# The second product by seven multiplications from block 42 instead of 50, its weight sums made in place and for four experts sooner

## The chip, the cores and the metric

The kernel runs on one core of a Trainium2 chip. The metric is the device time of one execution in microseconds (us); of several runs the median is given. The core has a matrix engine (TensorE, PE in the profile; its weight loads are listed apart as PEld), a vector engine (VectorE, DVE), an activation engine (ScalarE, ACT), a general engine (GpSimd, POOL) and a queue processor (SyncE, SP). SP and ACT issue most transfers, POOL the scatters by index.

## The reference

Two stages follow each other. The first is a mixing over the sequence by Fourier transform; the second sends each token to one of eight experts by a hash of its number.

```python
batch, seq, dim = (8, 2496, 256)
X = np.fft.rfft(x, axis=1)
y = np.fft.irfft(X * (filt_r + 1j * filt_i)[None], n=seq, axis=1)     # 8 x 2496 x 256, fp32
x = y.reshape(19968, 256)
expert = token_ids * 2654435761 % 8
for e in range(8):                                                   # w1: 256 x 1024, w2: 1024 x 256
    out[expert == e] = np.maximum(x[expert == e] @ w1[e], 0) @ w2[e]
```

All is fp32.

## The kernel before

**Tiles of tokens.** Tokens are sorted by expert while they are produced: the Fourier part scatters each row of its result to a place in a DRAM buffer `xs`, and every 256 places there (one tile, one expert) make one *block* of the second part. There are 85 tiles; 80 are always used (`NSURE`), 5 more only if the counts need them. The order of the tiles is fixed in five stages, since a tile can only be read when the batches are done from which its tokens come: blocks 0 to 9 need the first two batches, 10 to 19 three, 20 to 29 four, 30 to 49 six, 50 to 79 all eight. Within a stage even blocks go through one half of the experts and odd blocks through the other, so that an expert's weights, kept in one of two sets, mostly serve several blocks of the same parity; they are loaded again only where the expert changes (a condition on the transfer).

**A block** (`step`) computes a hidden tile of 1024 x 256 and an output tile of 256 x 256. The first product, `up` (line 881), is made by seven multiplications of half-size pieces instead of eight. For this POOL makes four differences of weight pieces for the block after (`weight_sums`, line 872, four subtractions), DVE makes four differences of token pieces (`token_sums`). The second product, `down` (line 918), is an ordinary product of 16 matmul calls of 256 columns. From block `WS` = 50 on, `late_step` (line 1047) takes the place of this with `both` (line 930): seven multiplications for the second product too, each of four matmul calls of 128 columns. Two names stand for the PE work of the two ways: rows `dps` at line 923 are `down`, rows `dne`, `dna`, `dnb`, `dnc` at line 950 are the seven. A matmul call of fp32 shows as two instructions.

**Sums of the second weights.** The seven multiplications need four 128 x 512 pieces per expert made from `w2`. `prepare(e, part)` (line 203) makes them once for each expert, on POOL, long before: part 0 loads `w2[e]` (1 MB) on SP into a buffer `raw` of the pool `xp`, which has two buffers and also serves the x tiles; parts 1 to 4 are four subtractions on POOL (row `mid<-raw`, line 199), from `raw` into a part of the tile `mid`; part 5 writes the result (1 MB) on SP to the DRAM buffer `t2s`. Blocks from `WS` on load them back with their weights (line 469), into the tiles `d_t` and `e_t`, the tables of the Fourier part, which are free once its last middle stage is over; `both` also keeps its token pieces and its sums `s` in the tile of the filter.

**The Fourier part** goes on beside the blocks. A batch has three parts, cut into pieces: `stage1` (loads x, first transform), `forward` and `back` (middle, with the filter), `stage3` (last transform, whose rows POOL scatters to `xs`, four scatters a piece). Their loads are `load1`, `load2`, `load4` on SP, their writes to DRAM are issued by ACT. A list `todo` gives each piece a due time in blocks; `run_until(t)` issues what is due, at five points of a block: after `up`, at three points inside `down`, and at the end. In a block from 50 on it is not called, since nothing is left by then. A stage 3 piece is eight matmuls of 256 columns, two ACT copies and four scatters on POOL.

**Order and waits.** Each engine and each queue runs its instructions in the order in which they stand. POOL's order in a block is: the weight differences for the block after, the two scatters of the block before (`store`, line 1012), then what `run_until` brings. SP's order has the loads of w1 (line 464) and w2 (line 467) two blocks ahead, and between them the loads of the pieces. Token tiles (`load`, line 836: four transfers `xg`, one `no`) are issued by ACT. In the built program SP's and ACT's transfers take eight semaphores in turn, and the issue of a transfer waits until the previous one with its semaphore has landed, whichever queue issued that.

```python
for e in range(E):
    t = 34.3 + 1.5 * e
    todo += within([(t + d, lambda e=e, k=k: prepare(e, k)) for k, d in enumerate((0, 1.1, 1.4, 1.7, 2, 2.3))])
```

`within` moves the due time into the second half of its block.

Of the kernel before, what the change touches and what calls it, by code (L numbers as in the profile page):

```python
# [11 lines left out]
F32 = mybir.dt.float32  # L12
# [7 lines left out]
P = 128  # L20
B, S, C = 8, 2496, 256
# [26 lines left out]
FP = F // P  # L48
# [2 lines left out]
NPAD = NT * TB - N  # L51
NQP = NPAD // P
NSURE = NT - 5
WS = 50

# [68 lines left out]
def kernel(  # L126
# [10 lines left out]
    nc = tc.nc  # L137
# [9 lines left out]
    t2_dram = nc.dram_tensor("t2s", (E, P, FP * C), F32)  # L147

    def pool(stack, name, bufs, space=None):
        kw = {} if space is None else {"space": space}  # L150
        return stack.enter_context(tc.tile_pool(name=name, bufs=bufs, **kw))
# [5 lines left out]
    xpool = pool(ctx, "xp", 2)  # L157
    ppool = pool(ctx, "pp", 3)
    t4pool = pool(ctx, "t4", 2)
# [16 lines left out]
    mid = cpool.tile([P, 10, SG * C], F32)  # L176
# [21 lines left out]
    def minus(eng, out_, a, b, op=OP.subtract):  # L198
        eng.tensor_tensor(out_, a, b, op=op)

    raw = {}

    def prepare(e, part):

        to = mid[:, 5 + 2 * (e % 2):7 + 2 * (e % 2), :].rearrange("p a b -> p (a b)")
        if part == 0:
            raw[e] = xpool.tile([P, FP, C], F32, name=f"raw_{e}", tag="x")
            nc.sync.dma_start(out=raw[e][:], in_=moe_w2[e].rearrange("(fp p) c -> p fp c", p=P))
        elif part < 5:
            b11, b12, b21, b22 = [raw[e][:, 4 * f:4 * f + 4, P * c:P * c + P] for f in range(2) for c in range(2)]  # L210
            t = [to.rearrange("p (k f c) -> p k f c", k=4, c=P)[:, k] for k in range(4)]
            k = part - 1
            minus(nc.gpsimd, t[k], (b12, b22, b22, b21)[k], (b11, t[0], b12, t[1])[k])
        else:
            nc.sync.dma_start(out=t2_dram[e], in_=to)

    put_off = {2: [], 3: []}

# [227 lines left out]
    def weights(i, which):  # L446

        if i >= NT:
            return
        if i >= 2 and which == 0:  # L450
            ws[i] = ws[i - 2][0:2]
        eng, kw = nc.sync, {}
        if which == 0:
            ws[i].append(eng.value_load(chunk_i[0:1, 0, i:i + 1], min_val=0, max_val=E - 1))
            if i >= 2:
                ws[i].append(eng.value_load(chunk_i[0:1, 1, i:i + 1], min_val=0, max_val=1))
        e = ws[i][2]
        if i >= 2:
            kw = {"cond": ws[i][3]}
        if which == 0:  # L460


            for f in (slice(0, F // 2), slice(F // 2, F)) if i < 2 else (slice(0, F),):
                eng.dma_start(out=ws[i][0][:, :, f],
                              in_=moe_w1[bass.ds(e, 1)].rearrange("one (p dp) f -> p (one dp) f", p=P)[:, :, f], **kw)
        else:
            eng.dma_start(out=ws[i][1], in_=moe_w2[bass.ds(e, 1)].rearrange("one (fp p) d -> p (one fp) d", p=P), **kw)
            if WS <= i < NSURE:
                eng.dma_start(out=late["t2"][i % 2].rearrange("p k f c -> p (k f c)"),
                              in_=t2_dram[bass.ds(e, 1)].rearrange("one p k -> p (one k)"), **(kw if i >= WS + 2 else {}))  # L470

# [254 lines left out]
    def within(todo, share=.5):  # L726

        return [(t // 1 + .5 + t % 1 * share, piece) for t, piece in todo if t is not None]
# [69 lines left out]
    todo = [(t - 200, piece) for t, piece in head]  # L798
    todo += [(t, lambda k=k: pads(k)) for k, t in enumerate((10.9, 11.6, 11.9, 16.9, 17.6, 17.95, 22.9))]

    def batch(b, t1, t2, t3):

        a1, a2, a3 = spaced(*t1, NU), spaced(*t2, N_2), spaced(*t3, NU)
        x0, d0, e0 = t1[0] - 2.5, t2[0] - 1.2, t3[0] - 1.2
        out = part2(b, a2, [max(d0, a2[2 * g] - 2.2) for g in range(NS // SG)], .6)
        out += part3(b, a3, [max(e0, a3[2 * v] - 2.2) for v in range(NV)])
        if b > 2:
            out += part1(b, a1, [max(x0, a1[2 * v] - 2.5) for v in range(NV)])
        return out
# [3 lines left out]
    todo += part2(3, spaced(6.4, 10, N_2), [5.2, 5.4, 5.6, 6.5, 7.5], .6)  # L813
    todo += part3(3, spaced(12, 16, NU), [11.2, 11.4, 12.5])
    todo += batch(4, (7.5, 11), (12.4, 16.4), (18.3, 22.3)) + batch(5, (13, 17), (18.4, 21.6), (23.2, 26.8))
    todo += batch(6, (20, 24), (26, 32), (34, 40)) + batch(7, (29, 34), (35.5, 40), (41.6, 47))
    for e in range(E):
        t = 34.3 + 1.5 * e
        todo += within([(t + d, lambda e=e, k=k: prepare(e, k)) for k, d in enumerate((0, 1.1, 1.4, 1.7, 2, 2.3))])
    todo.sort(key=lambda t: t[0])  # L820
    pre = [t for t in todo if t[0] < 0]
    main = [t for t in todo if t[0] >= 0]
# [107 lines left out]
    def both(i, ht):  # L930

        w1, w2 = ws[i][0:2]
        x, st, t = parts[i], parts[i]["sums"], sums[i]
        t2, s, one = late["t2"][i % 2], late["sums"], late["one"]
        h11, h12, h21, h22 = [ht[:, h, 4 * f:4 * f + 4, :] for h in range(2) for f in range(2)]
        b11, b12, b21, b22 = [w2[:, 4 * f:4 * f + 4, P * c:P * c + P] for f in range(2) for c in range(2)]
        half = F // 2

        def bank(k, name):
            p, tag = (banks[k], k) if k in banks else (fps, "f")  # L940
            return p.tile([P, 4, P], F32, name=f"{name}_{i}", tag=tag)

        def product(ps, w, xx, first):
            for f in range(4):
                nc.tensor.matmul(out=ps[:, f, :], lhsT=w[:, f * P:(f + 1) * P], rhs=xx,  # L945
                                 start=first and f == 0, stop=True, skip_group_check=True)

        def second(ps, a, b, first):
            for f in range(4):
                nc.tensor.matmul(out=ps[:, 0, :], lhsT=a[:, f, :], rhs=b[:, f, :],  # L950
                                 start=first and f == 0, stop=True, skip_group_check=True)

        def relu(out, in_):
            nc.scalar.activation(out=out, in_=in_, func=AF.Relu)  # L954

        def plus(out, ps, other):
            nc.vector.tensor_tensor(out, ps, other, op=OP.add)  # L957

        a, b, c = [bank(k, "up" + k) for k in "abc"]
        g, e = bank("f", "upg"), bank("f", "upe")  # L960
        if i + 1 < NSURE:
            token_parts(i + 1, late["xt"][i % 2])
        product(a, w1[:, 0, 0:half], x[0, 0], True)
        nc.scalar.copy(out=h21, in_=a[:])
        ask(i)
        product(b, t[1], st[:, 1, :], True)
        plus(h12, b[:], h21)
        product(g, t[2], st[:, 2, :], True)
        plus(h21, g[:], h12)
        product(c, t[0], st[:, 0, :], True)  # L970
        plus(h22, c[:], h21)
        relu(h22, h22)
        product(e, t[3], x[1, 1], True)
        plus(h21, e[:], h21)
        relu(h21, h21)
        product(a, w1[:, 1, 0:half], x[0, 1], False)
        relu(h11, a[:])
        minus(nc.vector, s[:, 0], h21, h22, OP.add)
        product(c, w1[:, 1, half:], st[:, 3, :], False)
        plus(h12, c[:], h12)  # L980
        relu(h12, h12)
        weights(i + 2, 0)

        e, a = bank("b", "dne"), bank("d", "dna")
        b, c = bank("f", "dnb"), bank("f", "dnc")
        rows[i] = outs.tile([P, 2, C], F32, name=f"osb_{i}", tag="osb") if i + 1 < NSURE else late["last"]
        o11, o12, o21, o22 = [rows[i][:, h, P * k:P * k + P] for h in range(2) for k in range(2)]
        second(e, h22, t2[:, 3], True)
        second(c, s[:, 0], t2[:, 0], True)
        second(a, h11, b11, True)  # L990
        nc.scalar.copy(out=one, in_=a[:, 0, :])
        minus(nc.vector, s[:, 1], s[:, 0], h11)
        minus(nc.vector, s[:, 2], h11, h21)
        minus(nc.vector, s[:, 3], h12, s[:, 1])
        second(b, s[:, 1], t2[:, 1], True)
        if i + 1 < NSURE:
            token_sums(i + 1, late["st"][i % 2], range(2))
        plus(o22, c[:, 0, :], one)
        plus(o21, e[:, 0, :], one)
        plus(o12, b[:, 0, :], one)  # L1000
        second(a, h12, b21, False)
        nc.scalar.copy(out=o11, in_=a[:, 0, :])
        if i + 1 < NSURE:
            token_sums(i + 1, None, range(2, 4))
        second(b, s[:, 2], t2[:, 2], False)
        plus(o22, b[:, 0, :], o22)
        plus(o21, b[:, 0, :], o21)
        second(c, s[:, 3], b22, False)
        plus(o12, c[:, 0, :], o12)
        weights(i + 2, 1)  # L1010
# [32 lines left out]
    def run_until(t):  # L1043
        while main and main[0][0] < t:
            main.pop(0)[1]()
# [9 lines left out]
    def step(i):  # L1055
        if i >= WS:
            late_step(i)
# [74 lines left out]
```

## Time and profile before

| | us |
|---|---|
| median of 3 runs (1415.62 to 1419.44) | 1417.82 |
| the profiled execution, its own time | 1415.08 |
| span of the profiled execution, first to last instruction | 1413.3 |
| start of block 0 (ACT copies its first product) | 140.2 |
| start of block 26, 42, 50 | 646.2, 916.4, 1029.8 |
| a block of the first kind with nothing of the Fourier part in it (47, 48, 49) | 13.16 |
| a block of the second kind (51 and later) | 12.51 |

The beginning of a block is read at one instruction, ACT's copy of the first product (line 899, or 964 in a block of the second kind), so the time from one to the next is one block. The engines are busy for these shares of the span: PE 97%, PEld 90%, DVE 63%, POOL 59%, ACT 29%. Sections of the page that follow name, for each group of instructions, its line, engine and operand tiles, its count, its total and mean duration, and what ended the idle time before it. A view by stretches gives the busy times of all engines between two moments, with the share of time in which the 16 DMA engines moved data.

### The profile page before, as it was taken

The numbers are of one execution on the slowest core, as the hardware profiler recorded it, in microseconds if no ns is written. First come the engines' busy times: TensorE is split into PE (matmuls) and PEld (weight loads), VectorE is DVE, ScalarE is ACT, GpSimd is POOL, SyncE is SP. The second block draws the span as 40 slices with busy tenths as digits, with TensorE's granted clock in tenths as the row PEclk, the third lists the DMA queues.
The fourth block names the chain that finished last, engine by engine and source line by source line (L and its number), as shares of the span: only waits on it lengthen the run. The fifth ranks groups of instructions, "written<-read, shape, count | busy, mean of one in ns | idle before, by whom it ended". The sixth has DMA issues, their size and how long they took to land.

```text
span 1413.3 us, 26363 instructions
## 1 busy us (share of the span) xinstructions
PE 1369.3 (97%) x9426; PEld 1271.4 (90%) x9426; DVE 891.9 (63%) x1636; ACT 416.0 (29%) x760; POOL 828.0 (59%) x736
## 2 busy tenths in 40 slices
PE   8999899999999999999999999999999999999997
PEld 7777888988888988899999899999999999999997
DVE  7773584575556576445765477657666777676775
ACT  4554122223232223232222222222222222222222
POOL 6267243743665565587533687798855556655563
PEclk9999999999999999999999999999999999999999
DMA  8677854867887698888755775887732525161621
GB/s 227 208 239 224 246 177 121 284 198 242 252 266 228 188 308 271 250 282 260 228 164 141 222 252 181 238 240 239 257 119 74 184 75 192 42 223 40 215 46 35
DMA packets 244505, 278.33 MB, mean 197 GB/s; under 512 B 125171, under 2 KB 213670, under 8 KB 234948
## 3 DMA queue, kind: packets, MB, share of 16 engines
q1 hardware_dynamic: 95149, 179.33, 40.2%
q10 hardware_dynamic: 129303, 52.69, 15.4%
q0 software_dynamic: 19920, 44.59, 9.0%
q8 instruction: 77, 1.26, 0.4%
q14 instruction: 56, 0.46, 0.1%
HBM read 293.65 MB, written 86.15 MB: 269 GB/s over the span
## 4 chain that ended last, share of the span: by engine, by line
PE 82%; DMA 8%; DVE 4%; issue 2%; ACT 1%; POOL 1%; ACTq 1%; SPq 0%; POOLq 0%; DVEq 0%
PE dps L923 20%; PE up_b L888 8%; PE up_a L888 5%; PE up_c L888 5%; PE pd L267 4%; PE dnc L950 4%; PE dnb L950 4%; PE dna L950 4%; PE upc L945 4%; PE upa L945 4%; PE pb L312 4%; PE pa L267 3%; PE pc L335 3%; PE upe L945 2%; PE upb L945 2%
## 5 line engine op out<-in xcount | busy, mean ns | idle before, releaser
L923 PE MATMUL dps<-wts,ht 128*128 128x256 f32 x1600 | 367.0, 380 | 1.5 <-ACT ht L892 1.5
L923 PEld LDWEIGHTS dps<-wts,ht 128*128 128x128 f32 x1600 | 302.0, 190 | 44.8 <-ACT ht L892 2.7
L1015 POOL DMA_INDIRECT out_dram<-osb,no x158 | 165.2, 1045 | 221.5 <-DVE osb L957 142.7
L433 POOL DMA_INDIRECT xs<-o,sidx x176 | 176.3, 1002 | 163.6 <-ACT o L269 68.4
L878 POOL TENSOR_TENSOR tw<-wts 128x512 f32<-128x512 f32 x158 | 204.1, 1292 | 111.3 <-DMA wts<-in_moe_w_dram 87.1
L878 POOL TENSOR_TENSOR tw<-wts,tw 128x512 f32<-128x512 f32 x158 | 205.8, 1303 | 6.2
L895 DVE TENSOR_TENSOR ht<-up_b,ht 128x512 f32<-128x512 f32 x150 | 103.6, 691 | 116.9 <-PE up_b L888 91.8
L892 ACT ACTIVATE ht<-ht 128x512 f32<-128x512 f32 x150 | 94.3, 630 | 185.2 <-DVE ht L895 165.3
L322 DVE TENSOR_TENSOR z<-pb,filt 64x512 f32<-64x512 f32 x160 | 110.2, 689 | 26.9 <-PE pc L335 24.9
L928 DVE COPY osb<-dps 128x512 f32<-128x512 f32 x50 | 34.5, 691 | 145.5 <-PE dps L923 145.2
L888 PE MATMUL up_a<-xt,wts 128*128 128x128 f32 x800 | 114.8, 276 | 7.3 <-ACT ht L899 4.0
L888 PEld LDWEIGHTS up_a<-xt,wts 128*128 128x128 f32 x800 | 105.2, 192 | 11.0 <-ACT ht L899 4.9
L888 PE MATMUL up_b<-st,tw 128*128 128x128 f32 x800 | 107.7, 278 | 3.8 <-DVE ht L895 2.5
L888 PEld LDWEIGHTS up_b<-st,tw 128*128 128x128 f32 x800 | 98.1, 193 | 6.3 <-issue 5.7
L895 DVE TENSOR_TENSOR ht<-up_c,ht 128x512 f32<-128x512 f32 x100 | 69.0, 690 | 37.5 <-PE up_c L888 32.9
L954 ACT ACTIVATE ht<-ht 128x512 f32<-128x512 f32 x90 | 56.5, 630 | 120.6 <-DVE ht L957 75.1
L338 ACT COPY mid<-pc 128x512 f32<-128x512 f32 x60 | 35.0, 583 | 155.0 <-PE pc L335 97.0
L267 PE MATMUL pd<-t,wi_t 120*117 120x256 f32 x320 | 75.9, 379 | 3.3 <-DMA t<-d 3.3
L318 DVE TENSOR_TENSOR y<-pb,filt 128x512 f32<-128x512 f32 x80 | 55.1, 689 | 34.1 <-PE pb L312 31.8
L323 DVE TENSOR_TENSOR y<-y,z 128x512 f32<-128x512 f32 x80 | 73.6, 920 | 2.7
L312 PE MATMUL pb<-mid,d_t 128*128 128x256 f32 x280 | 72.9, 383 | 1.5 <-DVE z L322 1.5
L269 ACT COPY o<-pd 117x512 f32<-117x512 f32 x80 | 44.9, 584 | 99.3 <-PE pd L267 48.7
(210 smaller groups left out, 2426.2 us busy)
## 6 DMA issues: line engine op xcount, KB each, us to landing
wts<-in_moe_w_dram SPq DMA_DIRECT2D x162, 1024.0 KB
xg<-xs ACTq DMA_DIRECT2D x321, 64.0 KB
mid<-d SPq DMA_DIRECT2D x70, 256.0 KB
d<-mid ACTq DMA_DIRECT2D x60, 256.0 KB
d_t<-t2s SPq DMA_DIRECT2D x15, 1024.0 KB
e_t<-t2s SPq DMA_DIRECT2D x15, 1024.0 KB
x<-in_x_dram SPq DMA_DIRECT2D x39, 312.0 KB
t<-d SPq DMA_DIRECT2D x12, 960.0 KB
```

Source lines behind the costliest of these rows:

```text
L267: nc.tensor.matmul(out=ps[0:cols * H, k, :], lhsT=w[:], rhs=src[:, 2 * i + k, :], start=True, stop=True)
L312: nc.tensor.matmul(out=ps[:, i, :], lhsT=d_t[:, s, :], rhs=rhs, start=True, stop=True)
L322: nc.vector.tensor_tensor(out=z[b], in0=ps[a], in1=f_t[1][64 * hi:64 * hi + 64, s1:s1 + 2, :], op=OP.mult)
L433: st = nc.gpsimd.indirect_dma_start(out=xs[:], out_offset=bass.IndirectOffsetOnAxis(ap=index, axis=0), in_=rows, in_offset=None, bounds_ch ...
L878: eng.tensor_tensor(t[k][:], p, q, op=OP.subtract)
L888: nc.tensor.matmul(out=ps[bank][:, f, :], lhsT=w[:, f * P:(f + 1) * P], rhs=xx, start=first and f == 0, stop=True, skip_group_check=True)
L892: nc.scalar.activation(out=out, in_=in_, func=AF.Relu)
L895: nc.vector.tensor_tensor(out, ps[bank][:], other, op=OP.add)
L923: nc.tensor.matmul(out=ps[:, h, :], lhsT=ht[:, h, fp, :], rhs=w2[:, fp, :], start=(fp == 0), stop=(fp == FP - 1))
L945: nc.tensor.matmul(out=ps[:, f, :], lhsT=w[:, f * P:(f + 1) * P], rhs=xx, start=first and f == 0, stop=True, skip_group_check=True)
L950: nc.tensor.matmul(out=ps[:, 0, :], lhsT=a[:, f, :], rhs=b[:, f, :], start=first and f == 0, stop=True, skip_group_check=True)
L1015: st = nc.gpsimd.indirect_dma_start(out=out[:], out_offset=bass.IndirectOffsetOnAxis(ap=to_rows[i][:, h:h + 1], axis=0), in_=o[:, h, :], i ...
```

## The change

- `WS` goes from 50 to 42: blocks 42 to 49 become blocks of the second kind.
- `prepare` works in place. The four quarters of `w2[e]` are loaded into one buffer by four transfers of 256 KB instead of one of 1 MB, the four subtractions overwrite the buffer, and the result is written from it. Nothing goes through `mid`.
- For experts 0 to 3 the buffer comes from the pool `t4` (two buffers, used for stage 3), and they are due from 26.4 on, 1.2 blocks apart; experts 4 to 7 use `xp` and are due from 33.4 on, 1.3 blocks apart. Before, all eight were due from 34.3 on, 1.5 apart.
- Batch 6's middle is due at 25.5 to 31.5 (before 26 to 32), its stage 3 at 33.6 to 39.6 (34 to 40); batch 7's stage 1 at 28.5 to 33 (29 to 34), its middle at 34 to 38.8 (35.5 to 40), its stage 3 at 40.6 to 46.6 (41.6 to 47).
- `both` calls `run_until(i + 1)` between its first and its second product, so that the stage 3 pieces due in blocks 42 to 45 run there.

```diff
-WS = 50
+WS = 42
@@ def prepare(e, part):
-        to = mid[:, 5 + 2 * (e % 2):7 + 2 * (e % 2), :].rearrange("p a b -> p (a b)")
         if part == 0:
-            raw[e] = xpool.tile([P, FP, C], F32, name=f"raw_{e}", tag="x")
-            nc.sync.dma_start(out=raw[e][:], in_=moe_w2[e].rearrange("(fp p) c -> p fp c", p=P))
+            p = t4pool if e < 4 else xpool
+            raw[e] = p.tile([P, FP, C], F32, name=f"raw_{e}", tag="t4" if e < 4 else "x")
+            w = raw[e][:].rearrange("p k c -> p (k c)").rearrange("p (k f c) -> p k f c", k=4, c=P)
+            src = moe_w2[e].rearrange("(fp p) c -> p fp c", p=P)
+            for k, (f, c) in enumerate(((0, 0), (1, 1), (0, 1), (1, 0))):
+                nc.sync.dma_start(out=w[:, k], in_=src[:, 4 * f:4 * f + 4, P * c:P * c + P])
         elif part < 5:
-            b11, b12, b21, b22 = [raw[e][:, 4 * f:4 * f + 4, P * c:P * c + P] for f in range(2) for c in range(2)]
-            t = [to.rearrange("p (k f c) -> p k f c", k=4, c=P)[:, k] for k in range(4)]
-            k = part - 1
-            minus(nc.gpsimd, t[k], (b12, b22, b22, b21)[k], (b11, t[0], b12, t[1])[k])
+            w = raw[e][:].rearrange("p k c -> p (k c)").rearrange("p (k f c) -> p k f c", k=4, c=P)
+            to, p, q = ((0, 2, 0), (2, 1, 2), (1, 1, 0), (3, 3, 1))[part - 1]
+            minus(nc.gpsimd, w[:, to], w[:, p], w[:, q])
         else:
-            nc.sync.dma_start(out=t2_dram[e], in_=to)
+            w = raw[e][:].rearrange("p k c -> p (k c)").rearrange("p (k n) -> p k n", k=4)
+            nc.sync.dma_start(out=t2_dram[e].rearrange("p (k n) -> p k n", k=4), in_=w)
...
-    todo += batch(6, (20, 24), (26, 32), (34, 40)) + batch(7, (29, 34), (35.5, 40), (41.6, 47))
+    todo += batch(6, (20, 24), (25.5, 31.5), (33.6, 39.6)) + batch(7, (28.5, 33), (34, 38.8), (40.6, 46.6))
     for e in range(E):
-        t = 34.3 + 1.5 * e
-        todo += within([(t + d, lambda e=e, k=k: prepare(e, k)) for k, d in enumerate((0, 1.1, 1.4, 1.7, 2, 2.3))])
+        t = 26.4 + 1.2 * e if e < 4 else 33.4 + 1.3 * (e - 4)
+        todo += within([(t + d, lambda e=e, k=k: prepare(e, k)) for k, d in enumerate((0, 1.1, 1.3, 1.5, 1.7, 1.9))])
@@ def both(i, ht):
         weights(i + 2, 0)
+        run_until(i + 1)
```

## The prediction, made before the changed kernel was run

> **What bounds the kernel now.** I read four views in this order: the page's shares and its chain that ended last, the stretches block by block, the chain inside single blocks, and the timeline where a block is longer than its matmuls.
>
> ```profile
> PE 1369.3 (97%) x9426; PEld 1271.4 (90%) x9426; DVE 891.9 (63%) x1636; ACT 416.0 (29%) x760; POOL 828.0 (59%) x736
> ...
> PE 82%; DMA 8%; DVE 4%; issue 2%; ACT 1%; POOL 1%; ACTq 1%; SPq 0%; POOLq 0%; DVEq 0%
> ```
>
> PE is at 97%, its weight loads at 90%, and 82% of the chain is PE. Most of the 8% of DMA lies before block 0 (140 us). Inside the blocks the kernel is a queue of matmuls, so a change pays by the matmul time it removes and by the waits of PE it removes or makes. The stretches below are blocks 27, 28, 29, 33, 43, 49, 50 and 51.
>
> ```profile
> 663.16:679.71 16.55, 16.55 (x106) 15.31 (x105) 11.89 (x19) 4.13 (x7) 10.88 (x10) 1.00 0.67 224
> 679.71:694.60 14.89, 14.89 (x98) 13.86 (x97) 9.15 (x15) 3.55 (x6) 6.80 (x6) 1.00 0.89 267
> 694.60:714.77 20.17, 20.17 (x123) 18.40 (x122) 13.76 (x19) 6.47 (x11) 8.60 (x9) 1.00 0.49 149
> ...
> 765.76:782.53 16.77, 16.10 (x108) 14.34 (x106) 5.75 (x11) 3.48 (x8) 7.90 (x7) 1.00 0.78 227
> ...
> 931.31:946.20 14.89, 14.89 (x99) 13.77 (x98) 7.86 (x12) 4.04 (x7) 13.23 (x13) 1.00 1.00 278
> 1016.64:1029.80 13.16, 13.16 (x91) 12.33 (x90) 6.01 (x12) 2.96 (x5) 4.53 (x5) 1.00 0.81 280
> 1029.80:1043.08 13.28, 12.72 (x114) 12.53 (x113) 10.16 (x21) 3.50 (x7) 8.28 (x8) 1.00 0.52 179
> 1043.08:1055.59 12.51, 12.51 (x114) 12.51 (x113) 8.56 (x21) 3.50 (x8) 7.32 (x7) 1.00 0.18 42
> ```
>
> After the length come the busy times of PE, PEld, DVE, ACT and POOL, then clock, DMA share and GB/s. A block of the first kind with nothing beside it is 13.16, of the second kind 12.51, both without a gap on PE. Block 43 holds one stage 3 piece more: 14.89 - 13.16 = 1.73 for 8 matmuls, 0.216 each, though DMA is at 1.00. With that price I can tell how much of blocks 26 to 41 is waiting: 916.42 - 646.22 = 270.2 long, 16 x 13.16 = 210.6 for the blocks, 260 Fourier matmuls x 0.216 = 56.2, so 3.4 remain. Of these, 2.7 lie in block 33 (16.77 against 13.16 + 4 x 0.216). Blocks 42 to 49 have 0.3, block 50 has 0.77 (13.28 against 12.51).
>
> ```profile
> 774.92 7.62 DMA xg<-xs
> 782.53 0.59 ACT ht L899
> ...
> 1007.86 0.89 PE up_b L888 x8
> 1008.75 6.91 PE dps L923 x32
> 1015.66 0.89 PE up_a L888 x8
> ```
>
> The lower lines give the removed work: `down` is 6.91, one product of 8 instructions is 0.89. The upper ones are block 33: ACT made its copy at 782.53, after an `xg` transfer. In the order of instructions with their waits, what stood ahead of that copy is the issue of `no` for tile 36, and it waits for a semaphore that SP's load of w1 for block 35 holds (1 MB, issued 770.32). ACT issued `no` at 782.10, and PE stood meanwhile. I call this a **hold**: a transfer of ACT queued behind a large one of SP. Its price here is 2.7.
>
> ```profile
> 1034.66 1.27 POOL L878 TENSOR_TENSOR tw<-wts,tw 128x512 f32<-128x512 f32 x1
> 1034.71 1.76 DVE L199 TENSOR_TENSOR filt<-ht 128x512 f32<-128x512 f32 x1 [0.70 <-ACT ht L954]
> ...
> 1036.52 0.97 PEld L950 LDWEIGHTS dnc<-d_t,filt 128*128 128x128 f32 x8 [0.75 <-DVE filt L199]
> ```
>
> Block 50's 0.77: the first sum of `both` took 1.76 on DVE, beside a subtraction on POOL, where the same row's median is 0.69, and `dnc` waited for it.
>
> **What the Trainium skill says.** "Perfetto Trace Analysis", Identifying the Most-Contended Engine: judge TensorE by weight loads, not matmul occupancy. The trace agrees: PEld goes from 12.33 of 13.16 to 12.51 of 12.51, and the block shrinks although PE reads full in both. "SBUF — State Buffer", Who interferes with whom: a DVE instruction with two SBUF inputs contends with a GpSimd instruction that reads SBUF, and one blocks. The 1.76 against 0.69 fits. "DMA: Bandwidth & Descriptors", Issuing engines are not separate DMA queues: all queues run on the same 16 engines. Block 33 shows ACT's issue waiting on SP's load, though by a semaphore of this program.
>
> **The change, part by part.**
>
> *Blocks 42 to 49.* Each loses 6.91 and gains seven times 0.89 = 6.24; the measured blocks give 13.16 - 12.51 = 0.65. Eight blocks: **-5.2**, all of it on the path, since PE has no gap in either kind. Their DVE rises from 6.01 to about 9 of 12.51: hidden.
>
> *Stage 3 pieces inside `both`.* Same 1.73 of PE, now between the products. ACT's two copies (0.585 each) come in 3.5 of 12.5 busy. POOL then has 4 x 1.29 differences, 2 stores and 4 scatters at 1.30 (their spacing in the timeline): 13.0 in a block of 12.51 + 1.73 = 14.24. It fits by 1.2, and its differences serve the next block, so lateness of some us is free. `run_until` also issues the last t4 load (block 42) on SP ahead of w2 for block 44, which has a block and a half: 0.
>
> *Start of the second kind.* The 0.77 leaves block 50. In block 42 the same sum has the 1.73 of the stage 3 piece ahead of `dne`, more than the 1.07 it was late. It can come back at block 46, the first without a piece. Half of it counted: **-0.4**.
>
> *In-place sums.* 32 subtractions before and after; the row `mid<-raw` has 1.26 to 1.61 each. Contiguous operands may gain nothing or up to 0.3 each; POOL in blocks 26 to 33 had 6 to 14 busy of 15 to 20. Taken as 0, at worst covered by that idle time. SP issues 24 transfers more at 0.41: 9.8 over 13 blocks, against waits of hundreds of us on SP: 0 by itself. The bytes are the same, the rows half as long. Price of one expert: load and store are 2.1 MB; queue 1 moved 179.33 MB in 40.2% of 1413.3, 316 GB/s, so 6.6 of all 16 engines; if the load went only as fast as queue 10 with its small packets (52.69 MB in 15.4%, 242 GB/s), 7.7. I take 6.6.
>
> *Experts 0 to 3 sooner.* 26.6 of DMA goes into blocks 27 to 31, 86.9 us with a mean share of 0.63: 0.63 + 0.31 = 0.94. Block 43 ran free at 1.00, so a full DMA alone doesn't stop PE; late transfers would. What waits there: SP stands before each store until POOL's last subtraction (before: 47.3 us in 6 waits, up to 16.9), with weights two blocks ahead and loads of batches 6 and 7 behind it; the buffers of experts 2 and 3 also wait for the stores of 0 and 1. These loads have about a block of slack. Every transfer issue from here on gets another of the eight semaphores: the hold in block 33 is probably gone (its `no` no longer stands behind a w1 load), others can arise, with ACT's `xg` and batch writes now behind quarters of `raw`. From below nothing, from above the rivals. I take -2.7 at one half, **-1.3**, and **+0.7** for a fuller DMA.
>
> *Second weight sums loaded sooner.* Experts change at blocks 44, 46, 47, 48, 50 and 51 (from the tokens); with the first two, 8 loads in place of 2: 6.3 MB, 20 of DMA in blocks 40 to 49. But some 3.6 experts' preparation leaves these blocks, 24. Nothing.
>
> *Earlier due times of batches 6 and 7.* Matmuls only change their block: 0. The shortest distance is batch 7's `load2` right behind its last stage 1 piece (blocks 32.9 and 32.6): SP stands there some us until the write has landed (estimated from the scatters of `o`, which land 2.9 to 5.0 after their issue), the first use is over a block later.
>
> Sum: -5.2 - 0.4 - 1.3 + 0.7 = **-6.2**. The profiled execution would take 1415.08 - 6.2 = 1408.9. It lies 2.7 below the median of the runs, so from the median: 1417.82 - 6.2 = **1411.6**. What a measurement of this kernel can tell from no change is about 0.3%, 4.25 us.
>
> **Rivals.**
>
> *DMA too full in blocks 27 and 28.* 0.67 + 0.31 and 0.89 + 0.31: the second goes over by 0.2 x 14.9 = 3.0, and one hold more comes with it (2.7, against the sum's 1.3 + 0.7 - 2.7). For it: blocks 22 and 23 at 0.93 and 0.97 lost 0.4. Against it: block 29 has room (0.49), and block 43. Gain about 6.2 - 3.0 - 1 = 2: 1415.8, no change that can be told.
>
> *The port between POOL and DVE.* If POOL stays late after the scatters, its differences meet DVE's sums in blocks 46 to 49 too: 4 x 0.77 = 3.1 lost, gain 3.1, 1414.7. Against it: 1.2 of room in each of blocks 43 to 45.
>
> *Holds at the preparations; slower.* The place is ACT's queue in blocks 28 to 40: its `xg`, `d1` and `d2` transfers are behind `raw` quarters and stores that wait for POOL. If half of the eight experts make one hold as in block 33, 4 x 2.7 = 10.8 stands against 6.2: 1422.4. It decides from three holds (8.1) on. Against it: before, eight preparations in blocks 34 to 47, with SP waits of up to 16.9, cost under 1.5 in all, since an `xg` is issued a half to a whole block after the load that it waits for.
>
> **How the numbers follow.** Forecast 0.72, DMA 0.17, port 0.05, slower 0.06. If every wait from 26 to 50 goes, 5.2 + 0.77 + 3.4 + 0.3 = 9.7: 1408.1, the low end. The first two rivals end at 1415.8; with one us for their rough prices the high end is 1417. Faster 0.72, within 0.22, slower 0.06.
>
> **What would show it.** Right: blocks 46 to 49 at 12.51, 43 and 44 at 14.24, block 42 without 0.77, row `dps` x1344 in place of x1600, `dnc` of 42 to 45 not waiting. Wrong in its main term: blocks 43 to 49 longer than this, with PE idle before `dnc` or `dnb`. The rivals: idle of PE in blocks 27 to 40 with ACT released by `xg`, or DMA at 1.0 over several blocks; `filt` sums of 1.7 in blocks 46 to 49.

## The result, and the profile after

| | before, us | after, us |
|---|---|---|
| median of 20 runs each, taken together | 1417.96 | 1414.01 |
| lowest to highest | 1412.63 to 1425.16 | 1407.74 to 1418.50 |
| span of the profiled execution | 1413.3 | 1411.7 |
| start of block 26, 42, 50 | 646.22, 916.42, 1029.80 | 647.30, 921.23, 1027.59 |

The ratio of the times is 0.9972, with a 95% interval of 0.996 to 0.9984: some 4 us faster, where 6.2 were forecast. Two later sets ran the changed kernel again and gave 0.9956 (0.9943 to 0.9969) and 0.9982 (0.997 to 0.9995). The forecast of 1411.6 is 2.4 us low; the measured time lies inside the range.

From the page of the changed kernel, the shares, the chain that ended last, and the row of the ordinary second product:

```profile
PE 1367.1 (97%) x9618; PEld 1273.8 (90%) x9618; DVE 907.8 (64%) x1708; ACT 419.4 (30%) x776; POOL 831.4 (59%) x736
...
PE 79%; DMA 10%; DVE 6%; issue 3%; POOL 1%; ACT 1%; ACTq 0%; SPq 0%; POOLq 0%; DVEq 0%
...
L926 PE MATMUL dps<-wts,ht 128*128 128x256 f32 x1344 | 312.2, 381 | 3.0 <-ACT ht L895 3.0
```

Row `dps` has x1344, as the change says: eight blocks fewer with 32 instructions each. PE still has 97%. What is new is DVE's share of the chain, 6% where it was 4%: in some place matmuls now wait for DVE.

The stretches show where. They are blocks 27, 28, 29, 33, 35, 36, 43, 49, 50 and 51 of the changed kernel; the columns are those explained in the prediction.

```profile
665.04:682.52 17.48, 17.48 (x114) 16.25 (x113) 13.93 (x19) 4.13 (x7) 14.16 (x12) 1.00 0.88 293
682.52:699.53 17.01, 16.33 (x99) 14.69 (x99) 9.84 (x15) 4.49 (x8) 7.95 (x7) 1.00 0.89 285
699.53:717.82 18.29, 18.29 (x114) 16.80 (x113) 13.25 (x19) 5.20 (x9) 13.89 (x12) 1.00 0.98 296
768.00:782.95 14.95, 14.95 (x99) 13.85 (x98) 5.84 (x12) 4.04 (x8) 4.85 (x5) 1.00 0.67 190
801.29:820.61 19.32, 18.52 (x114) 16.69 (x113) 16.46 (x20) 5.19 (x10) 13.87 (x12) 1.00 0.59 181
820.61:840.12 19.51, 18.57 (x114) 16.74 (x113) 16.93 (x21) 5.00 (x9) 16.51 (x14) 1.00 0.87 255
935.41:949.65 14.24, 14.24 (x122) 13.97 (x121) 9.84 (x22) 4.46 (x10) 12.16 (x12) 1.00 0.73 223
1015.09:1027.59 12.50, 12.50 (x114) 12.50 (x113) 8.19 (x20) 3.49 (x7) 7.26 (x6) 1.00 0.90 295
1027.59:1040.66 13.07, 12.78 (x114) 12.59 (x114) 9.79 (x21) 3.50 (x8) 7.27 (x7) 1.00 0.63 202
1040.66:1053.16 12.50, 12.50 (x114) 12.50 (x113) 8.79 (x21) 3.49 (x7) 7.29 (x7) 1.00 0.19 44
```

Block 43 has 14.24 and block 49 has 12.50, both without a gap on PE: this is the intended gain, in full. In blocks 35 and 36 PE stands for 0.8 and 0.9 us, while DVE is busy for 16.46 and 16.93. A block with the same matmuls in the kernel before, block 36 there, has 18.29 with DVE busy for 12.72:

```profile
813.58:831.87 18.29, 18.29 (x114) 16.77 (x113) 12.72 (x19) 5.10 (x10) 15.60 (x14) 1.00 0.75 249
```

DVE has hardly more work, 20 and 21 instructions in these two stretches against 19. Single instructions of it take longer.

The timeline of the changed kernel inside block 36 (start, duration, engine, line, operation; in brackets the idle time before it and what ended that) shows which ones:

```profile
821.00 1.02 POOL L436 DMA_INDIRECT xs<-o,sidx  x1 [4.41 <-issue]
...
824.92 0.99 POOL L436 DMA_INDIRECT xs<-o,sidx  x1 [0.30 <-issue]
...
825.92 1.31 POOL L199 TENSOR_TENSOR raw<-raw 128x512 f32<-128x512 f32 x1
...
827.16 1.29 POOL L881 TENSOR_TENSOR tw<-wts 128x512 f32<-128x512 f32 x1
...
827.31 1.30 DVE L872 TENSOR_TENSOR st<-xt 128x128 f32<-128x128 f32 x1
...
828.53 1.27 POOL L881 TENSOR_TENSOR tw<-wts,tw 128x512 f32<-128x512 f32 x1
828.64 1.30 DVE L872 TENSOR_TENSOR st<-st,xt 128x128 f32<-128x128 f32 x1
...
829.76 1.31 POOL L881 TENSOR_TENSOR tw<-wts 128x512 f32<-128x512 f32 x1
829.87 1.35 DVE L872 TENSOR_TENSOR st<-xt 128x128 f32<-128x128 f32 x1
...
831.03 1.31 POOL L881 TENSOR_TENSOR tw<-wts,tw 128x512 f32<-128x512 f32 x1
831.14 1.36 DVE L872 TENSOR_TENSOR st<-xt,st 128x128 f32<-128x128 f32 x1
...
832.42 0.68 DVE L321 TENSOR_TENSOR y<-pb,filt 128x512 f32<-128x512 f32 x1
833.11 1.39 DVE L325 TENSOR_TENSOR z<-pb,filt 64x512 f32<-64x512 f32 x2
...
834.65 1.09 PE L270 MATMUL pd<-t,wi_t 120*117 120x256 f32 x4 [0.94 <-DVE z L325]
```

Read it from above. The block began at 820.61, and POOL begins it with the four scatters of the stage 3 piece of block 35 (the first and the last are shown). So its weight differences `tw` start at 827.16, and there they meet DVE's four token sums `st`. Each `st` begins just after a `tw` and ends about 0.15 after it: 1.30 to 1.36 instead of the 0.29 that it has alone. The four take some 4 us more. Behind them on DVE stand `y` and `z`, the filter steps of a `forward` piece, which read a PSUM buffer that PE wants for `pd`; PE stands 0.94. (ACT too stands in this block, 8.22 before a copy at 836.01, behind `xg`. But it stands 7.88 in the same place, at 838.52, in block 36 of the kernel without these waits that is shown below.)

How far all blocks 26 to 41 are affected follows from the prediction's own sum: after, they take 921.23 - 647.30 = 273.9; less 16 x 13.16 and 264 Fourier matmuls x 0.216 there remain **6.3 us of waiting, where before had 3.4**. (Before there were 260. Eight came from blocks 42 to 49, and four left for block 25.)

### The profile page after: what moved, and what is told of

Same layout as the page of the kernel before. It is cut to its first block, busy times and chain, and to the rows that moved or that the text cites. A ratio compares the mean times of both kernels' runs of the same rounds, so it can differ in the third digit from the quotient of the medians.

```text
span 1411.7 us, 26945 instructions
## 1 busy us (share of the span) xinstructions
PE 1367.1 (97%) x9618; PEld 1273.8 (90%) x9618; DVE 907.8 (64%) x1708; ACT 419.4 (30%) x776; POOL 831.4 (59%) x736
## 3 DMA queue, kind: packets, MB, share of 16 engines
q8 instruction: 79, 1.29, 0.4%
## 4 chain that ended last, share of the span: by engine, by line
PE 79%; DMA 10%; DVE 6%; issue 3%; POOL 1%; ACT 1%; ACTq 0%; SPq 0%; POOLq 0%; DVEq 0%
PE dps L926 16%; PE up_b L891 6%; PE dnc L953 5%; PE dna L953 5%; PE dnb L953 5%; PE upa L948 5%; PE upc L948 4%; PE up_a L891 4%; PE pd L270 4%; PE up_c L891 4%; PE pb L315 3%; PE pa L270 3%; PE pc L338 3%; PE upe L948 2%; PE upb L948 2%
## 5 line engine op out<-in xcount | busy, mean ns | idle before, releaser
L926 PE MATMUL dps<-wts,ht 128*128 128x256 f32 x1344 | 312.2, 381 | 3.0 <-ACT ht L895 3.0
L926 PEld LDWEIGHTS dps<-wts,ht 128*128 128x128 f32 x1344 | 255.0, 191 | 40.5 <-ACT ht L895 3.6
L898 DVE TENSOR_TENSOR ht<-up_b,ht 128x512 f32<-128x512 f32 x126 | 87.1, 692 | 98.6 <-PE up_b L891 75.5
L891 PE MATMUL up_a<-xt,wts 128*128 128x128 f32 x672 | 97.3, 278 | 5.5 <-DVE xt L859 3.6
L891 PEld LDWEIGHTS up_a<-xt,wts 128*128 128x128 f32 x672 | 89.1, 193 | 8.4 <-issue 3.8
L891 PE MATMUL up_b<-st,tw 128*128 128x128 f32 x672 | 90.3, 278 | 3.7 <-DVE ht L898 2.7
L891 PEld LDWEIGHTS up_b<-st,tw 128*128 128x128 f32 x672 | 82.4, 193 | 5.8 <-issue 5.6
L953 PE MATMUL dna<-wts,ht 128*128 128x128 f32 x608 | 80.4, 275 | 0.0
L948 PE MATMUL upa<-filt,wts 128*128 128x128 f32 x592 | 78.2, 275 | 0.0
L199 DVE TENSOR_TENSOR filt<-ht 128x512 f32<-128x512 f32 x76 | 57.4, 756 | 26.4 <-ACT ht L957 26.4
```

The source lines that it names most:

```text
L891: nc.tensor.matmul(out=ps[bank][:, f, :], lhsT=w[:, f * P:(f + 1) * P], rhs=xx, start=first and f == 0, stop=True, skip_group_check=True)
L898: nc.vector.tensor_tensor(out, ps[bank][:], other, op=OP.add)
L926: nc.tensor.matmul(out=ps[:, h, :], lhsT=ht[:, h, fp, :], rhs=w2[:, fp, :], start=(fp == 0), stop=(fp == FP - 1))
```

## The experiments

The theory: the new due time of batch 6's stage 3, 33.6, puts every piece at .80 of its block, where 34 put it at .50, right behind `up`: the first is due at 33.80 instead of 34.50. The four scatters then run over the end of the block, POOL's differences start late, meet `st`, and PE waits. The rivals: the seven products from block 42 on cause it, POOL simply has too much work beside, or the in-place preparation costs it.

The first four kernels ran in a set in which the kernel before took 1457.97 (median of 43) and its first part alone is some 15 us longer; only ratios and blocks of that set are compared with each other.

### Batch 6's stage 3 back behind `up`

```diff
-... batch(6, (20, 24), (25.5, 31.5), (33.6, 39.6)) ...
+... batch(6, (20, 24), (25.5, 31.5), (34, 40)) ...
```

> The changed kernel with batch 6's stage 3 due at 34 to 40 as before, so that its pieces fall at .50 of a block (right behind the first product) and not at .80. Theory (phase): in the changed kernel the four scatters of a piece issued at .80 run over the block's end, POOL's weight differences start some 5 us late and meet DVE's token sums (row st, 1.2 to 1.35 us each in blocks 34 to 38 against 0.29 before); z and y come late and PE waits about 1 us in each of blocks 35 to 38. Then here st is back at 0.29 between 785 and 880 us, blocks 35 to 38 lose less than 1 us together instead of 4.3, and the time is 0.994 to 0.996 of before, against 0.9972 of the changed kernel. Rival (POOL has too much to do): the four subtractions for an expert every 1.3 blocks in place of 1.5 overfill POOL, whatever the phase: st stays above 1 us and blocks 35 to 38 lose 3 us or more. Rival (DMA): the waits come from a fuller DMA and stay as they are.

Measured: 1448.08, ratio to before 0.9941 (0.9917 to 0.9965). Blocks 35, 36, 37 and 38 take 18.28, 18.34, 20.08 and 17.85. Over blocks 33 to 41 it takes 150.46; the kernel of the next experiment, with the same pieces there and the late due time, takes 153.51. The `st` of blocks 34 to 38 (count: shortest, median and longest in ns), first one of three rows of this kernel, whose other two have medians of 292 and 283:

```profile
L872 DVE TENSOR_TENSOR st<-xt x10: 282/288/357, 820.9 to 895.9; 128x128 f32<-128x128 f32 x10
```

then the changed kernel, in its own set:

```profile
L872 DVE TENSOR_TENSOR st<-xt x10: 283/1216/1356, 789.6 to 868.0; 128x128 f32<-128x128 f32 x10
L872 DVE TENSOR_TENSOR st<-st,xt x5: 293/1241/1314, 790.0 to 866.8; 128x128 f32<-128x128 f32 x5
L872 DVE TENSOR_TENSOR st<-xt,st x5: 284/1354/1357, 790.4 to 869.3; 128x128 f32<-128x128 f32 x5
```

With only these due times undone, no `st` of this window is slow and the blocks are short. The theory held. All of POOL's work is still in this kernel, so its amount alone does not make the waits.

### The ordinary second product up to block 49

```diff
-WS = 42
+WS = 50
```

(an edit of the changed kernel)

> The changed kernel with WS back at 50: sums in place and sooner, due times of batches 6 and 7 as changed, but blocks 42 to 49 of the first kind. Theory: the eight blocks are worth 8 x 0.65 = 5.2 us and the rest of the change costs 1 to 2 us (hold in block 33 gone, -2.7; 4.3 in blocks 35 to 38, 0.9 each in 27 and 40), so this kernel is 1 us slower than before: ratio 0.9995 to 1.002. If instead the blocks brought less than their matmuls say, it stands at the changed kernel's 0.997 to 0.9985; if the earlier schedule is harmless, at 0.998 to 0.9995.

Measured: 1453.45, 0.9984 (0.9964 to 1.0004). The number missed: I had 0.9995 to 1.002, and 0.9984 lies where I had put a harmless schedule. The interval reaches into all the ranges named, so the number decides nothing. The blocks gave the answer that was asked for: blocks 46 to 49 have 13.16 again, while blocks 35 and 36 keep their 19.55 and 19.49, and `st<-xt` has a median of 1169 ns. So the new waits are not from the seven products, but from the earlier schedule.

### No subtractions for experts 4 to 7

```diff
         elif part < 5:
+            if e >= 4:
+                return
```

> The changed kernel without the four subtractions for experts 4 to 7 (their sums are left out; loads and stores stay). Phase theory: the scatters still run over the block's end and POOL's differences still begin about 4 us into the block, so part of the meeting with st stays: st medians 0.6 to 1.3 us between 785 and 880, blocks 35 to 38 lose 1.5 to 3.5 us. Rival (too much work on POOL): st is back at 0.29 and blocks 35 to 38 lose under 1 us. In both, the store of expert 7's sums no longer waits for POOL, so the wait of PE in block 40 for the stage 3 load behind it on SP (0.9) goes.

Measured, one run: 1448.66. The wait of block 40 is gone (14.89, as expected). Blocks 35 to 38, however, have 19.54, 20.25, 20.78 and 17.30, and blocks 33 to 41 take 154.49: no better than with all subtractions. So less work on POOL does not give the time back. But my theory's number was exceeded too, and its trace is not the same picture: here most `st` escape, as the rival had it,

```profile
L874 DVE TENSOR_TENSOR st<-xt x10: 277/292/1352, 820.7 to 899.7; 128x128 f32<-128x128 f32 x10
```

and the chain runs over ACT, whose copies stand behind transfers:

```profile
860.09 8.28 DMA d<-mid
...
871.25 1.08 ACT o L274 x2
872.33 0.50 ACT ht L904
...
872.87 0.71 PE up_a L893 x4
```

With the late pieces, taking away one wait let another one stand in its place. That the late phase costs is common to all kernels that have it. That it costs by `st` is what the traces of most of them show, not of this one, and no run separates `st` from everything else that the phase moves.

### Both stage 3 behind `up`

The first experiment, and batch 7 in the same manner:

```diff
-    ... (33.6, 39.6)) + batch(7, (28.5, 33), (34, 38.8), (40.6, 46.6))
+    ... (34, 40)) + batch(7, (28.5, 33), (34, 38.8), (41, 47))
```

> The changed kernel with batch 6's stage 3 due at 34 to 40 and batch 7's at 41 to 47, so that every stage 3 piece falls at .50. Theory (phase): as with batch 6's alone, blocks 34 to 40 lose under 1 us in place of about 5, st between blocks 34 and 39 is at 0.29; besides, the load for batch 7's first stage 3 piece is issued 0.2 block later and used 0.7 block later, so the 0.9 that PE waited for it in block 40 goes. Together 3.5 to 5 us faster than the changed kernel: 0.993 to 0.9955 of before, and 0.996 to 0.998 of the changed kernel beside it. If the phase only moved the waits elsewhere, it is within 1 us of the changed kernel.

> The kernel with both stages 3 at .50 a second time, beside the changed kernel, because the two medians of the last set (1412.02 of 7 runs, 1411.99 of 22) did not show the 3.2 us by which its trace is shorter from block 25 to 52. Phase theory: blocks 25 to 52 again 3 us shorter than in the changed kernel, 0.992 to 0.996 of before, 0.997 to 0.999 of the changed kernel. Rival (the blocks' gain is given back elsewhere): the trace shows the 3 us lost again before block 25 or after block 52, and the medians are equal within 1 us.

Measured twice: 0.995 (0.9929 to 0.9971; median 1412.02 against 1417.15) and 0.9944 (0.9927 to 0.9962; 1411.37 against 1419.08). The timeline of block 36, which begins here at 822.09, is the counterpart of the one shown above:

```profile
819.77 1.27 POOL L881 TENSOR_TENSOR tw<-wts 128x512 f32<-128x512 f32 x1
...
823.92 1.26 POOL L881 TENSOR_TENSOR tw<-wts,tw 128x512 f32<-128x512 f32 x1
...
828.80 0.32 DVE L872 TENSOR_TENSOR st<-xt 128x128 f32<-128x128 f32 x1
829.15 0.29 DVE L872 TENSOR_TENSOR st<-st,xt 128x128 f32<-128x128 f32 x1
...
830.77 1.01 POOL L436 DMA_INDIRECT xs<-o,sidx  x1 [1.82 <-ACT mid L341]
...
834.69 0.99 POOL L436 DMA_INDIRECT xs<-o,sidx  x1 [0.30 <-issue]
```

The differences end at 825.2, before `st` starts; the scatters come after it and end at 835.7, inside the block. The chain of the first of the two executions through blocks 35 to 38 is all but wholly PE (issue 0.3%). The waiting in blocks 26 to 41, by the same sum as above, is 2.6 and 3.3.

### The changed kernel again, for the comparison within one set

> The changed kernel once more, beside the others on the same chip: 0.996 to 0.9985 of before, with blocks 35 to 38 again some 4 us over their matmuls and st above 1 us there, if these waits belong to the kernel's order and not to one execution.

> The changed kernel beside it, a third time: 0.995 to 0.9985 of before, and 3 us longer from block 25 to 52 than the kernel with both stages 3 at .50.

Measured: the ratios given at the top, and in both traces the same long blocks: 19.26 and 19.26 in block 35, 19.50 and 19.50 in 36, waiting in 26 to 41 of 5.7 and 6.7. In the median, the kernel with both phases corrected beats it by 5 us in one set, and not at all in the other (1412.02 of 7 runs and 1411.99 of 22), which is what the expectation gave to waits that are only moved elsewhere. The traces speak against that: behind the start of block 52 the two kernels take 358.2 to 358.8 in all five executions. What differs is the part before block 25, 629.8 to 637.5 in executions of the changed kernel alone. So the blocks between are the steadier measure. From the start of block 25 to that of block 52, in which all kernels have the same Fourier work:

| kernel | block 25 to 52, us |
|---|---|
| before, two executions | 425.99, 425.36 |
| changed, three executions | 423.35, 422.67, 423.54 |
| both stage 3 behind `up`, two executions | 419.47, 420.26 |

The version with both phases corrected is 3.3 us shorter than the changed kernel and 5.8 shorter than the one before, near the 6.2 that the prediction gave to the change. The 3.3 is a little under the 3.5 to 5 first expected. Of it, 2.5 lie in blocks 33 to 41. Another 0.8 lie in blocks 26 to 32, where the two kernels do not differ yet: there single executions of the changed kernel had a wait in block 28 or 29. By the ratio, the kernel with batch 6's phase alone corrected (0.9941) cannot be told from this one.

### The kernel before, with the late phase

```diff
-... batch(6, (20, 24), (26, 32), (34, 40)) ...
+... batch(6, (20, 24), (26, 32), (34.6, 40.6)) ...
```

(an edit of the kernel before)

> The kernel before with one thing of the change: batch 6's stage 3 due at 34.6 to 40.6, so at .80 of a block (blocks 34 to 39). Phase theory: the scatters run over the block's end here too, st goes from 0.29 to over 1 us in blocks 35 to 39, and blocks 35 to 39 lose 2.5 to 5 us more than in the kernel before (there 0.8 in all): ratio 1.0015 to 1.004. Rival (it needs the sooner preparation with its quarters and stores, POOL or DMA being fuller): st stays mostly at 0.29 and the time is that of before within 1 us.

> The kernel before once more, for its trace on the same chip: block 33 again about 2.5 us over its matmuls (the hold), st at 0.29 from block 34 to 39.

Measured: 1429.73, ratio 1.0082 (1.0059 to 1.0105): slower, and by more than twice the upper end of what I expected. The kernel before in the same set, one run: 1416.97, with blocks as known. Blocks 33 to 41 take 162.81 against 150.04. The chain of the edited kernel in block 37:

```profile
847.88 2.24 DVE st L869
850.14 3.85 DVE st L869 x3
853.99 0.60 DVE y L318
...
856.03 3.36 DVE y L323
```

The same three `st` at 3.85 as in the changed kernel, and on top the `prepare` subtractions of this kernel meet `y`, which takes 3.36 where it has 0.69 alone. So the late due time alone does damage, without any other part of the change.

Of the 12.8, 9.3 lie in blocks 35 to 39. The other 3.4 lie in blocks 33 and 34, ahead of the first late scatters. There ACT's copy that begins block 34 comes late behind a write, `d<-mid`, with 10.35 us in the chain, and PE stands 2.42. The load of the first piece is due later here too; whether it lengthens this wait was not tried. The stretches of blocks 34 and 39 show one thing more:

```profile
789.32:805.39 16.07, 15.33 (x83) 14.07 (x84) 5.74 (x12) 4.03 (x8) 3.67 (x5) 0.89 0.72 216
883.25:905.17 21.92, 19.72 (x110) 16.91 (x109) 17.14 (x20) 4.77 (x9) 15.81 (x15) 0.92 0.52 169
```

The granted clock is 0.89 and 0.92 in them, where it is 1.00 in blocks 35 and 36 of the changed kernel. Behind the stand of 2.42 it was 0.50 from 792 to 794 us. So the loss of 12.8 here, against 2.5 there, has two visible parts beside the four `st`: the `prepare` subtractions that are due at that moment, and matmuls that take longer after the longer stands.

### In-place sums alone

The kernel before with `prepare` in place for all experts (all from `xp`), and the due times of before. The diff is the part of `prepare` shown above.

> The kernel before with only prepare as changed (four loads of 256 KB, subtractions in place, buffers from xp for all eight, due times as before). Theory: by itself nothing: the subtractions on POOL keep their 1.26 to 1.31, blocks 34 to 48 change by under 1 us in all; the hold in block 33 lies before the first load and stays (16.0 to 16.8). Rival (the 24 transfers more in the turn of eight semaphores make holds): some block from 34 to 47 is 1.5 us or more longer than before.

Measured, one run: 1414.63, span 1412.9; blocks 34 to 47 take 220.71 (220.95 in both traces of the kernel before), block 33 has 17.38, a little above the expected, so the in-place sums do not remove its wait. The subtractions have a median of 1.30. In place costs nothing and brings nothing.

### The hold in block 33

The load of w1 for block 35 cut from 1024 to 16 columns in the kernel before:

```diff
-... else (slice(0, F),):
+... else (slice(0, 16 if i == 35 else F),):
```

> The kernel before with one transfer made small: the load of w1 for block 35 brings 16 of 1024 columns, and the rest of that set keeps older weights (part of the computation is left out). Theory (hold): ACT's issue of no for tile 36 waits for the semaphore of that load, so block 33 goes from 16.77 to 14.0 to 14.2 us, with ACT's copy no longer late, and nothing else moves by more than 0.5 us. Rival (the token transfers themselves were late, or DMA was full): block 33 keeps 15.5 us or more.

Measured, one run: 1455.28. The stretch of block 33, with no gap on PE:

```profile
804.36:818.70 14.34, 14.34 (x94) 12.77 (x93) 9.10 (x11) 3.48 (x7) 7.06 (x6) 1.00 0.67 164
```

14.34 against 16.77 in the first profile of the kernel before (16.16 in the second), so the excess of some 2 us was a wait of ACT's queue for that large load, as the prediction had read it. (This kernel leaves most of that load out.)

### The pieces at the end of `both`

```diff
         weights(i + 2, 0)
-        run_until(i + 1)
...
+        run_until(i + 1)
         weights(i + 2, 1)
```

> The changed kernel with the pieces of blocks 42 to 45 behind the second product in place of between the two. Theory: the piece's 1.73 of PE between the products covers the first sum of both, which meets POOL's late differences in the first blocks (1.0 to 1.8 us on DVE in blocks 42 to 45 against 0.69); without this cover dnc waits, as it did in block 50 before: blocks 42 to 45 together 2 to 4 us longer than 56.3. Rival: POOL gets its scatters later and its differences in time, the first sum takes 0.69, and the blocks keep their 14.24.

Measured, one run: 1430.86. Blocks 42 to 45 take 15.45, 19.79, 18.06 and 19.19, 72.5 together, against 56.3 in the changed kernel: 16 more, where I expected 2 to 4. The chain in block 43:

```profile
941.35 2.25 DVE filt L199
...
944.12 1.22 DVE filt L199 x2
945.34 1.54 issue
946.88 1.75 DVE filt L199
...
949.81 1.16 PE dnb L953 x8
```

This is the late phase once more, in blocks of the second kind: the scatters move POOL's differences onto the sums of the second product, which `dnc` and `dnb` wait for directly. I had expected a meeting of the first sum alone; here all four are long. Of the 16, some 11.5 are stands of PE. The rest is busy time, 61.05 in these four blocks against 56.3, at a granted clock of 0.94 to 0.97. Against the end of the block, the call between the products is worth 16 us.

## Why the prediction was right or wrong

**Blocks 42 to 49, -5.2: exact.** They take 106.36 against 113.38, with eight stage 3 matmuls (1.73) fewer: -5.3. Blocks 43 and 44 have 14.24, blocks 46 to 49 12.50 or 12.51, and no row of `dnc` or `dnb` has idle time before it from block 42 to 49. POOL's room of 1.2 in such a block was enough.

**Block 50's 0.77, counted half: smaller.** Block 42 is free of it, as argued (14.18). But it did not move to block 46, it stayed in block 50, at 0.57. From the chain there:

```profile
1017.00 11.44 DMA xg<-xs
...
1032.90 1.16 DVE filt L199
```

The tiles from 50 on hold tokens of all batches. DVE begins block 50 with the transposing of the tokens for block 51, whose `xg` lands only at 1028.44; its sums come late behind that, and the first `filt` meets POOL again. -0.2 in place of -0.4 (-0.4 in one of the two repeats, where block 50 has 12.89).

**The hold in block 33, half of 2.7 counted: it went.** Block 33 has 14.95, its matmuls alone (13.16 + 8 x 0.216 = 14.89). That it was a hold is shown by the shortened load. It stayed with the in-place sums alone (17.38) and went with `WS` at 50 (15.01), so it is the new due times that remove it; by which of the moved transfers was not tried. So the term is -2.7 where -1.3 was counted. Others of about 1 us came in single executions: block 28 has 17.01 here and 16.52 and 16.17 in the repeats, block 29 has 19.47 in one.

**"Earlier due times of batches 6 and 7. Matmuls only change their block: 0." This step failed.** I followed the matmuls and SP's loads of these pieces, and not what they issue on POOL. POOL's room was worked out for blocks 43 to 45 only, where the piece runs between the products. The due time 33.6 in place of 34 reads like a shift of 0.4 block, but `within` makes it 33.80 in place of 34.50: four scatters now stand ahead of POOL's differences of block 34, where they stood behind them, and so on in each block after. With batch 7's stage 3, which is treated in the same way, it cost 2.5 us in blocks 33 to 41 (changed kernel against both phases corrected, at the same number of matmuls), and 3.1 with batch 6's alone, in the first set. So the terms for blocks 26 to 41, -1.3 + 0.7 + 0 = -0.6, measured +2.9, although the hold in block 33 went wholly.

**A store that waits for late subtractions.** Block 40 lost 0.9 (15.77; 15.65 and 15.56 in the repeats). From its chain:

```profile
889.53 0.35 SPq L218
...
890.07 9.81 DMA t<-d
...
899.92 1.99 PE pd L270 x8
```

SP stood at the store of expert 7's sums until POOL had made the last of them, and batch 7's stage 3 load, queued behind it, came late. The prediction named just this order, and took the load's slack for about a block. It was too little here: without the subtractions, and with batch 6's phase corrected, block 40 has 14.89.

**The sum in the trace.** -5.3 (42 to 49), -0.2 (50), +2.9 (26 to 41) make -2.6 from block 25 to 52, which is what the traces have (425.99 to 423.35). The medians give -3.95, with an interval of about -2.3 to -5.7, and hold this. That the time came out inside the range is in part luck: the hold brought 1.4 more than was counted for it, and so covered some of what the new waits took.

**The rivals.** The DMA in blocks 27 to 29 was at 0.88, 0.89 and 0.98, and no gap of PE over 0.2 us there is common to all executions: not borne out. Holds at the preparations, the slower case: none lasting. The port between POOL and DVE was the right mechanism in the wrong place: not at the `filt` sums of blocks 46 to 49 (mean 0.69 there), but at `st` in blocks 35 to 38.

**How the two engines meet.** The Trainium skill, "SBUF — State Buffer", Who interferes with whom, states that a DVE instruction with two SBUF inputs contends with a GpSimd instruction that reads SBUF. The traces agree: beside a subtraction on POOL, `st` goes from 0.29 to 1.36 and `filt` from 0.69 to 1.76, while a sum with one input in PSUM keeps its 0.69 (`ht<-up_b,ht` at 825.97 in the changed kernel, beside the `raw` subtraction of 825.92). How much is lost varies: a `filt` that begins in the last 0.1 of a subtraction keeps 0.69 (at 1296.84), and a `y<-y,z` was held over two. POOL's scatters did not slow such sums: with both phases corrected, the row `y<-y,z` at 834.77 has 0.69 beside the scatter at 834.69. They only put the subtractions in the wrong place.

**What stays open.** Block 62 takes 12.60 to 13.14 and block 68 12.74 to 13.32 in every kernel with `WS` = 42, and 12.50 in every kernel with `WS` = 50; some 1 us that the prediction did not have. In the changed kernel's block 68 the weights for 69 land late, so POOL's difference meets the first sum there. Why they land later was not settled. In the first set, blocks 41 to 46 lose up to a microsecond and more in kernels of both kinds; that was not settled either. For the kernel without the last four subtractions, what takes the place of the `st` waits was seen in one execution only.

## What to carry to other kernels

Where a piece of work moves, write down what it issues on every engine and what stands behind that, not only the engine that bounds the kernel: here four scatters of POOL, moved to the other side of four subtractions, cost 2.5 us of a gain of 5.8. A schedule in fractions is a phase: ask on which side of the next step's preparation it falls. When an effect of 3 us is looked for in a kernel whose executions differ by 10, compare the same blocks in several traces, and check the cause in both directions, by undoing it in the new kernel and by making it in the old one.

## What the runs showed of the hardware that was not expected

A small sum on DVE is held up by as much as a large one: `st`, 128 x 128 and 0.29 us alone, took up to 1.36 beside a subtraction on POOL of 1.29, and four in a row alternated with four subtractions, one for one: 5.3 us instead of 1.2. One sum of the same total size, `filt`, lost 1.1 beside one subtraction, and `y<-y,z` of 0.69 took 3.36 beside two. So in these traces several small instructions on DVE were worse off than one large one. A subtraction in place on contiguous quarters took 1.28 to 1.30 on POOL, the same as from strided ones into another tile (1.29). A stand of PE was sometimes followed by a further loss: behind one of 2.42, in the kernel before with the late phase, the granted clock was 0.50 for 2 us, and block 34 took 16.07 instead of 14.44. Behind the stands of 0.8 and 0.94 in the changed kernel it was 1.00, and behind one of 1.87 in block 37 of that other kernel too. What decides between these cases was not tried.
